# Exponentials that read PSUM in steps and write in order, instead of the reverse, in an attention and gated long-convolution kernel

## The chip, the cores and the metric

The kernel runs on one core of one Trainium2 chip. The metric is the device time of one launch in microseconds (us); before the change the median of three runs is 485.76 us (485.69 to 485.93). The core has a matrix engine (PE), which writes its results to PSUM, and three engines that work on tiles of 128 partitions: ACT (scalar engine: exponentials, copies), DVE (vector engine) and POOL. SP does no arithmetic here; it issues transfers. Each engine takes its own instructions in order, and the engines wait for one another through semaphores.

## The reference

Eight batches, 12 heads, 448 positions, 64 numbers a head. First comes an attention whose softmax has a one added to its denominator (with the maximum m taken out, that one is exp(-m)). Its result, laid out as 448 x 768 per batch, is projected to three streams; the second is convolved along the sequence with a long filter through a Fourier transform, and the three are multiplied and projected again.

```python
# q, k, v: (8, 12, 448, 64)
scores = scale * np.matmul(q, k.transpose(0, 1, 3, 2))
m = np.max(scores, axis=-1, keepdims=True)
e = np.exp(scores - m)
attn = e / (np.sum(e, axis=-1, keepdims=True) + np.exp(-m) + 1e-09)
x = np.matmul(attn, v)                      # then to (8, 448, 768)
x1, x2, x3 = split(x @ w_proj)              # three times 768
x2 = irfft(rfft(x2, axis=1) * rfft(filter_fft, axis=0), n=448, axis=1)
out = (x1 * x2 * x3) @ w_out
```

## The kernel before

**Attention.** The kernel works on pairs of heads: 6 pairs in each of 8 batches, 48 in all, numbered `i`. The maximum is not taken out. For a pair, the 448 keys of each of the two heads fall into three tiles of 128 keys and a rest of 64; the rests of both heads share a fourth tile. `scores(t)` (L767 to L774) lets PE write scores with the keys on the partitions and the queries along the row: for t = 1, 2, 3 two matmuls fill a pair of PSUM banks, one bank for each head, 448 floats in each; for t = 0 one matmul fills one bank with the shared rest. `exps(t)` (L776 to L791) is one ACT instruction that reads these scores from PSUM, applies the exponential and writes bf16 to SBUF: into `e` (896 elements on 128 partitions, a ring of six tiles) for t = 1, 2, 3, and into `er` (448 elements, a ring of two) for t = 0. PE then multiplies `e` and `er` with `vn`, the values with a column of ones (`out_rest`, L811; `out_rests`, L803), taking 128 columns of `e` at a time, that is 128 queries in row order. DVE adds one to the sum, takes its reciprocal and scales (`norm`, L824 to L826), into `xb`.

**Order of the queries.** A row of `e` must hold the queries in row order, 0 to 447. The queries are loaded four rows to a partition (NST = 4), so after transposing, column j * 112 + n of `qT` is query 4n + j. In batches 0 and 1 (`b < NSTAGED`, `staged`) PE transposes q into PSUM, and the copy back (`q_back`, L494 on DVE, once L492 on ACT) reads PSUM in the order (n j), so that `qT` is in row order. In batches 2 to 7 (`loaded`) DMA transposes write `qT` and `kT` (L533, L540) and the columns stay in the order (j n); the scores have that order as well, and the exponentials bring it to row order. The access patterns that do so are all that the change touches.

**The rest.** The scaled result is transposed by DMA (L896; by PE at L905 for most pairs of batch 0). `dense(b)` then folds the sequence into even and odd parts (DVE, L957 and L962), projects (PE L985, copies L997 and L999), applies the Fourier tables (L1012, copies L1020), multiplies by the filter's spectrum (L1026, L1032), transforms back (L1097, copy L1106, DVE L1115 to L1126), computes the two gates (PE L1058, ACT L1070, DVE L1073), multiplies (L1141), projects out (PE L1170, ACT L1182) and stores (SP L1189, L1192).

**Order of the work.** A planner (`Plan`) runs while the kernel is built: every task has an engine, a cost, a wanted time, what it needs and what it makes and which buffers it takes and gives. It emits the tasks in one fixed order for each engine, and gives out PSUM's eight banks; at most two pairs of banks hold scores ("sc") at a time. The exponentials are tasks on ACT with a written-down cost of 0.81 (`e`) and 0.44 (`er`), and those figures are the same in both versions. Attention of later batches is interleaved with `dense` of earlier ones.

**Transfers.** SP issues nearly all loads (q at L562, k and v at L584, the rests at L548), the transposes and the stores, in one order. The loads land in small rooms as float32, and POOL casts them to bf16 (L568 for q, L589 for k, L601 for v); a room is free for the next load after its cast.

Of the kernel before, what the change touches and what calls it, by code (L numbers as in the profile page):

```python
# [21 lines left out]
NST = S // SP  # L22
# [234 lines left out]
def kernel(  # L257
# [97 lines left out]
    def bank(hy):  # L355
        i = plan.banks[hy][0]
        return psum[:, 512 * i : 512 * i + 512]
# [5 lines left out]
    def pair(hy):  # L363
        i = plan.banks[hy][0]
        return psum[:, 512 * i : 512 * i + 1024].rearrange("p (u n) -> p u n", u=2)
# [394 lines left out]
    def attention(i):  # L760
# [15 lines left out]
        def exps(t):  # L776
            if t:
                P["e"][t] = e = es[(3 * i + t - 1) % 6]
                to, of = e[:, 0 : 2 * S], pair(("sc", ("S", i, t)))[:, :, 0:S]
                if b < NSTAGED:  # L780
                    to = to.rearrange("p (u n) -> p u n", u=2)
                else:
                    to = to.rearrange("p (u n j) -> p u j n", u=2, j=NST)
                    of = of.rearrange("p u (j n) -> p u j n", j=NST)
                nc.scalar.activation(to, of, AF.Exp, scale=SCALE)  # L785
            else:
                P["e"][t] = e = er[i % 2]
                to, of = e[:, 0:S], bank(("hy", ("S", i, t)))[:, 0:S]
                if b >= NSTAGED:
                    to, of = to.rearrange("p (n j) -> p j n", j=NST), of.rearrange("p (j n) -> p j n", j=NST)  # L790
                nc.scalar.activation(to, of, AF.Exp, scale=SCALE)  # L791

        def out_banks():
# [52 lines left out]
        for t in range(4):  # L846
            w = tau(i, t / 4 if i or t else 1.0)
            ex = with_rests(i - 1) if t == host else dict(cost=0.0, emit=lambda: None, need=[], make=[], take=[], give=[])
            if t == 0 or b == 0:

                def one(t=t, ex=ex):
                    scores(t)
                    ex["emit"]()

                add("PE", (0.4 if t else 0.19) + ex["cost"], w, one,
                    need=[("kT", i), ("qT", i)] + ([("S", i - 1, 2)] if b else []) + ([] if i or t else ["kT0"]) + ex["need"]
                    + ([("S", i, t - 1) if t > 1 else ("S", i - 1, 3)] if t and (i or t > 1) else []),
                    make=[("S", i, t)] + ex["make"], take=[(ring(t), ("S", i, t))] + ex["take"], give=ex["give"])
            elif (3 * i + t) % 2 == 0:

                old = (i, t - 1) if t > 1 else (i - 1, 3)

                def both(pair=(old, (i, t)), ex=ex):
                    for j, n in pair:
                        T[j]["scores"](n)
                    ex["emit"]()

                add("PE", 0.6 + ex["cost"], tau(old[0], old[1] / 4), both,
                    need=[("kT", old[0]), ("qT", old[0]), ("kT", i), ("qT", i)] + ex["need"]
                    + [("S", old[0], old[1] - 1) if old[1] > 1 else ("S", i - 1, 3)],  # L870
                    make=[("S",) + old, ("S", i, t)] + ex["make"],
                    take=[("sc", ("S",) + old), ("sc", ("S", i, t))] + ex["take"], give=ex["give"])
            add("ACT", 0.81 if t else 0.44, w - 1.0, lambda t=t: exps(t), need=[("S", i, t)],
                make=[("e", i)], take=[("e" if t else "er", (i, t))], give=[(ring(t), ("S", i, t))])
# [465 lines left out]
```

## Time and profile before

| | |
|---|---|
| median of three runs | 485.76 us |
| the profiled execution, its own time | 484.45 us |
| its span, first to last instruction | 482.7 us |
| mean granted clock of PE | 0.975 |
| bytes moved by DMA | 64.43 MB, 133 GB/s over the span |
| attention pair 12 (first of batch 2), first score matmul | 74.0 us |
| last exponential begins | 424.7 us |

The profile is of one execution. A group of instructions is named by its line, its engine and operation, and what it writes and reads; `e<-psum` is an instruction that writes a tile `e` from PSUM. "Busy" is the time in which an engine runs instructions; the last part of such a line is the time in which the engine was idle just before them, and which instruction ended the wait. PEld is PE's loading of weights, which runs beside its matmuls.

### The profile page before, as it was taken

Reading aid. Unit: us, or ns where it says so; the run is one execution under the profiler, and the core shown is the slowest. Engines: PE = TensorE matmul, PEld = TensorE weight load, DVE = VectorE, ACT = ScalarE, POOL = GpSimd, SP = SyncE. Lnnn points to the kernel's source line nnn. Section 1 sums busy time; section 2 is a strip of 40 time slices with the busy share of each in tenths; the row PEclk is TensorE's granted clock in tenths of the full one; section 3 lists DMA queues with packets and bytes.
Section 4 is the critical chain, followed back from the end, with each engine's and each line's share of the span. In section 5 each row is a group of like instructions: output and inputs, shape, how many; then the busy total and the mean of one; then the engine's idle time right before and its main releaser. Section 6 shows DMA issues by size and latency. Waiting matters only on the chain.

```text
span 482.7 us, 9536 instructions
## 1 busy us (share of the span) xinstructions
PE 391.6 (81%) x3700; PEld 242.0 (50%) x3700; DVE 254.0 (53%) x667; ACT 405.3 (84%) x460; POOL 107.4 (22%) x240
## 2 busy tenths in 40 slices
PE   8987996798596777677787987687779887789996
PEld 7655753464343454335453653444346443556653
DVE  5666586556273255392582645435128551387761
ACT  6784889969969999999979699998999989964453
POOL 6736324161333230342313211000000000000000
PEclk9998999899989999999999899899899998999999
DMA  8999968994976995993965403282110113010013
GB/s 233 244 230 238 202 151 189 185 260 105 242 148 170 223 190 151 211 239 73 245 148 139 168 16 116 61 128 67 70 29 2 34 67 98 1 35 1 34 65 132
DMA packets 116333, 64.43 MB, mean 133 GB/s; under 512 B 73085, under 2 KB 112704, under 8 KB 116288
## 3 DMA queue, kind: packets, MB, share of 16 engines
q1 hardware_dynamic: 111568, 58.18, 50.3%
q0 software_dynamic: 4480, 5.41, 6.6%
q8 instruction: 29, 0.48, 0.4%
q10 hardware_dynamic: 240, 0.23, 0.1%
q14 instruction: 16, 0.13, 0.1%
HBM read 43.86 MB, written 11.01 MB: 114 GB/s over the span
## 4 chain that ended last, share of the span: by engine, by line
ACT 41%; PE 36%; issue 8%; DMA 7%; DVE 4%; POOL 2%; SPq 1%; ACTq 0%; POOLq 0%; DVEq 0%
ACT e L785 29%; PE psum L1058 15%; PE psum L985 7%; PE psum L1170 6%; ACT er L791 4%; DMA nat<-in_k_dram 4%; PE psum L811 3%; ACT osb L1182 3%; PE psum L772 2%; DMA nat<-in_q_dram 1%; ACT x L1070 1%; ACT cr L1106 1%; PE psum L1097 1%; ACT xs L1020 1%; PE psum L1012 1%
## 5 line engine op out<-in xcount | busy, mean ns | idle before, releaser
L785 ACT ACTIVATE e<-psum 128x896 bf16<-128x896 f32 x144 | 260.6, 1921 | 15.0 <-PE psum L772 15.0
L1058 PE MATMUL psum<-xT,wproj_bf 128*128 128x448 bf16 x576 | 128.1, 363 | 11.6 <-ACT e L785 7.7
L1058 PEld LDWEIGHTS <-wproj_bf 128*128 128x128 bf16 x576 | 55.3, 100 | 61.6 <-issue 22.3
L985 PE MATMUL psum<-wproj_bf,xf 128*113 128x384 bf16 x384 | 71.1, 331 | 4.1 <-ACT e L785 3.7
L772 PE MATMUL psum<-qT,kT 64*128 64x448 bf16 x288 | 44.5, 358 | 23.9 <-ACT e L785 22.0
L1170 PE MATMUL psum<-wout_bf,yT 128*128 128x384 bf16 x288 | 54.7, 328 | 10.7 <-ACT e L785 6.6
L985 PEld LDWEIGHTS <-xf 128*113 128x113 bf16 x384 | 50.9, 134 | 22.9 <-issue 10.6
L791 ACT ACTIVATE er<-psum 128x448 bf16<-128x448 f32 x48 | 52.6, 1096 | 2.6 <-PE psum L774 2.5
L1026 DVE TENSOR_TENSOR t<-xs,hrs 113x768 bf16<-113x768 bf16 (+1 forms) x64 | 34.7, 577 | 30.5 <-ACT xs L1020 30.5
L824 DVE TENSOR_SCALAR rec<-psum 128x8 f32<-128x8 f32 x48 | 7.8, 162 | 79.7 <-PE psum L811 79.2
L811 PE MATMUL psum<-vn,e 128*128 128x65 bf16 x1152 | 46.7, 197 | 0.0
L1073 DVE TENSOR_TENSOR g<-x,psum 128x448 bf16<-128x448 bf16 x48 | 29.6, 616 | 28.9 <-PE psum L1058 18.4
L1170 PEld LDWEIGHTS <-yT 128*128 128x128 bf16 x288 | 27.7, 98 | 31.8 <-issue 14.8
L811 PEld LDWEIGHTS <-e 128*128 128x128 bf16 x1152 | 41.2, 100 | 3.3 <-issue 0.7
L1070 ACT CAST x<-psum 128x448 bf16<-128x448 f32 x48 | 27.6, 574 | 16.5 <-PE psum L1058 16.4
L1182 ACT COPY osb<-psum 128x384 f32<-128x384 f32 x56 | 28.5, 530 | 14.5 <-PE psum L1170 14.0
L772 PEld LDWEIGHTS <-kT 64*128 64x128 bf16 x288 | 12.1, 94 | 49.2 <-issue 47.6
L568 POOL CAST nat<-nat 112x512 bf16<-112x512 f32 x36 | 22.9, 643 | 56.0 <-DMA nat<-in_q_dram 55.9
L826 DVE TENSOR_TENSOR xb<-psum,rec 128x512 bf16<-128x512 f32 x48 | 33.2, 691 | 1.7
L601 POOL CAST vn<-nat 128x192 bf16<-128x192 f32 x58 | 21.4, 390 | 45.2 <-PE psum L811 42.2
L1020 ACT CAST xs<-psum 113x384 bf16<-113x384 f32 (+1 forms) x64 | 29.4, 527 | 2.0 <-PE psum L1012 1.9
L997 DVE CAST x<-psum 113x384 bf16<-113x384 f32 x32 | 17.6, 551 | 23.9 <-PE psum L985 23.8
(111 smaller groups left out, 446.8 us busy)
## 6 DMA issues: line engine op xcount, KB each, us to landing
nat<-in_q_dram SPq DMA_DIRECT2D x47, 224.0 KB, 4.5
out_dram<-osb SPq DMA_DIRECT2D x24, 384.0 KB, 2.4
nat<-in_k_dram SPq DMA_DIRECT2D x41, 192.0 KB, 4.3
nat<-in_v_dram SPq DMA_DIRECT2D x41, 192.0 KB, 4.7
wproj_bf<-in_moe_w_proj_dram POOLq DMA_DIRECT2D x2, 1152.0 KB, 17.1
rests<-in_k_dram SPq DMA_DIRECT2D x8, 192.0 KB, 4.9
rests<-in_v_dram SPq DMA_DIRECT2D x8, 192.0 KB, 5.1
out_dram<-osb SPq DMA_DIRECT2D x8, 192.0 KB, 2.7
```

Of the source, the lines that this page charges most:

```text
L772: nc.tensor.matmul(sc[:, u, 0:S], kT[b % 2][c, hp, t, :], qT[b % 2][c, hp, :])
L785: nc.scalar.activation(to, of, AF.Exp, scale=SCALE)
L791: nc.scalar.activation(to, of, AF.Exp, scale=SCALE)
L811: nc.tensor.matmul(out_bank(u)[:, n, :], P["e"][1 + t][:, u * S + n * 128 : u * S + n * 128 + 128], vn[b % 2][:, hp, 4 * u + t, :], start= ...
L826: nc.vector.tensor_tensor(W["xb", b][:, hp].rearrange("p n (u d) -> p u n d", u=2), op[:, :, :, 0:DH], rec[:].unsqueeze(3).to_broadcast([1 ...
L985: nc.tensor.matmul(pps[:FQ, :DCH], W["xf", b][:, pg, kt, 0:FQ], wproj_bf[:, kt, D + ch * DCH : D + (ch + 1) * DCH], start=(kt == 0), stop= ...
L1020: nc.scalar.copy(L["xs", par, ch][:K, pg % 2, :], L["Z", pg, ch][:K, :DCH])
L1026: nc.vector.tensor_tensor(t[:K], L["xs", par, ch][:K], h, op=ALU.mult)
L1058: nc.tensor.matmul(p[:, :S], wproj_bf[:, kt, 2 * part * D + dt * 128 : 2 * part * D + (dt + 1) * 128], xT()[:, kt, 0:S], start=(kt == 0), ...
L1070: nc.scalar.copy(L["x1", dt], p[:, :S])
L1170: nc.tensor.matmul(ops[:n, :DCH], y[:, dt, 0:n], wout_bf[:, dt, ch * DCH : (ch + 1) * DCH], start=(dt == 0), stop=(dt == NDT - 1),)
L1182: nc.scalar.copy(L["os", st][:n, ch * DCH : (ch + 1) * DCH], L["O", st, ch][:n, :DCH])
```

## The change

In `exps`, for batches 2 to 7 only, the order in which the instruction walks through its elements is changed. Before, it took the scores in the order in which they lie in PSUM (j, then n) and wrote each at its place in the row, four bf16 elements (8 bytes) after the one before it. Now it takes them in row order (n, then j): it reads PSUM in steps of 112 floats, four to a run, then goes one float on, and writes one element after the other. The same elements arrive at the same places. Batches 0 and 1 are not touched.

```diff
                 if b < NSTAGED:
                     to = to.rearrange("p (u n) -> p u n", u=2)
                 else:
-                    to = to.rearrange("p (u n j) -> p u j n", u=2, j=NST)
-                    of = of.rearrange("p u (j n) -> p u j n", j=NST)
+                    to = to.rearrange("p (u n j) -> p u n j", u=2, j=NST)
+                    of = of.rearrange("p u (j n) -> p u n j", j=NST)
                 nc.scalar.activation(to, of, AF.Exp, scale=SCALE)
             else:
                 P["e"][t] = e = er[i % 2]
                 to, of = e[:, 0:S], bank(("hy", ("S", i, t)))[:, 0:S]
                 if b >= NSTAGED:
-                    to, of = to.rearrange("p (n j) -> p j n", j=NST), of.rearrange("p (j n) -> p j n", j=NST)
+                    to, of = to.rearrange("p (n j) -> p n j", j=NST), of.rearrange("p (j n) -> p n j", j=NST)
                 nc.scalar.activation(to, of, AF.Exp, scale=SCALE)
```

## The prediction

> **What bounds the kernel now.** I began with the page's busy shares and its costliest groups, to see which engine is full and with what.
>
> ```profile
> PE 391.6 (81%) x3700; PEld 242.0 (50%) x3700; DVE 254.0 (53%) x667; ACT 405.3 (84%) x460; POOL 107.4 (22%) x240
> ...
> L785 ACT ACTIVATE e<-psum 128x896 bf16<-128x896 f32 x144 | 260.6, 1921 | 15.0 <-PE psum L772 15.0
> ...
> L772 PE MATMUL psum<-qT,kT 64*128 64x448 bf16 x288 | 44.5, 358 | 23.9 <-ACT e L785 22.0
> ...
> L791 ACT ACTIVATE er<-psum 128x448 bf16<-128x448 f32 x48 | 52.6, 1096 | 2.6 <-PE psum L774 2.5
> ```
>
> ACT and PE are both over 80% busy, and the exponentials (L785, L791) are 313 of ACT's 405 us. The mean of 1921 ns hides two prices, which the view of the single line shows, with the waits that it causes.
>
> ```profile
> L785 ACT ACTIVATE e<-psum x144: 912/2216/2377, 8.5 to 424.7; 128x896 bf16<-128x896 f32 x144
> ...
>   PE psum L772: 22.0, 29
>   PE psum L803: 8.3, 6
>   PE psum L1058: 7.7, 6
> ```
>
> The shortest takes 912 ns and the median 2216 ns, for the same 896 elements. The timeline of ACT says which is which: batches 0 and 1 (before 75 us) are the short ones, batches 2 to 7 the long ones.
>
> ```profile
> 57.87 1.73 ACT L785 ACTIVATE e<-psum 128x896 bf16<-128x896 f32 x2
> 59.47 0.56 ACT L791 ACTIVATE er<-psum 128x448 bf16<-128x448 f32 x1
> 59.90 0.51 ACT L1020 CAST xs<-psum 113x384 bf16<-113x384 f32 x1
> ```
>
> ```profile
> 79.33 1.26 ACT L791 ACTIVATE er<-psum 128x448 bf16<-128x448 f32 x1
> 80.32 0.64 ACT L1106 CAST cr<-psum 128x452 bf16<-128x452 f32 x1
> 80.85 0.54 ACT L1070 CAST x<-psum 128x448 bf16<-128x448 f32 x1
> 81.27 4.18 ACT L785 ACTIVATE e<-psum 128x896 bf16<-128x896 f32 x2
> 85.17 1.08 ACT L1106 CAST cr<-psum 128x452 bf16<-128x452 f32 x2
> ```
>
> From start to next start, an early pair takes 59.47 - 57.87 = 1.60 us (0.80 each), a late pair 85.17 - 81.27 = 3.90 us (1.95 each); an early `er` 0.43 us, a late one 0.99 us. Last I read busy time by stretch: 75 us is where the late exponentials begin, 424.7 us where the last one starts.
>
> ```profile
> 30.00:75.00 45.00, 39.73 (x449) 26.83 (x448) 30.72 (x79) 32.00 (x56) 15.96 (x31) 0.96 0.96 195
> 75.00:139.00 64.00, 49.38 (x429) 28.97 (x430) 33.77 (x84) 55.68 (x57) 21.85 (x45) 0.95 0.94 201
> 139.00:188.50 49.50, 37.30 (x357) 22.43 (x354) 20.23 (x52) 47.64 (x47) 16.42 (x35) 1.00 0.73 173
> 188.50:253.60 65.10, 49.05 (x480) 29.39 (x477) 39.28 (x102) 60.53 (x59) 19.98 (x43) 1.00 0.79 183
> 253.60:424.70 171.10, 136.86 (x1247) 81.68 (x1245) 74.60 (x200) 160.20 (x158) 12.26 (x28) 0.96 0.27 70
> 424.70:482.70 58.00, 52.39 (x357) 32.29 (x355) 35.46 (x93) 26.67 (x55) 0.00 (x0) 1.00 0.17 55
> ```
>
> Columns: length, then busy PE, PEld, DVE, ACT, POOL, then granted clock, DMA share, GB/s. From 75 to 424.7 us (349.7 us) ACT is busy 324.1 us (93%) and PE 272.6 us (78%). Before and after it PE is full: 39.7 of 40.5 us, leaving out 4.5 us in which it waits for a POOL cast (98%), and 52.4 of the 54.1 us up to its last matmul (97%). So the late exponentials set the pace of the middle, and nothing else there.
>
> **Price of a late exponential after the change.** Its write to SBUF becomes contiguous, which the early ones show at 912 and 538 ns. New is the read: PSUM in steps of 112 floats, runs of four. No exponential here reads so. The nearest rows are the copies of `qT` for batches 0 and 1, which read PSUM in the same (n j) order, from bf16 words 112 elements apart, and write plainly.
>
> ```profile
> L492 ACT COPY qT<-psum x1: 567/567/567, 24.6 to 24.6; 128x448 bf16<-128x448 bf16 x1
> ...
> L912 ACT COPY xT<-psum x2: 527/530/532, 32.2 to 36.1; 128x448 bf16<-128x448 bf16 x2
> ...
> L494 DVE COPY qT<-psum x11: 612/624/626, 7.5 to 60.1; 128x448 bf16<-128x448 bf16 x11
> ```
>
> On ACT the scattered read takes 567 ns against 530 for the plain one of the same count: 37 ns per 448 elements, so 74 ns for 896. On DVE it takes 624 against 386 ns (plain copy at L914): 238 ns more, 0.53 ns an element. Low end: nothing more, 0.80 us effective. High end by DVE's row: 0.80 + 0.48 = 1.28 us, and 0.43 + 0.24 = 0.67 us for `er`. A gain below the plain row is excluded, as the element count and the output are the same. I take ACT's own row, rounded to 0.85 and 0.46 us, since it is the same engine and the same order of reading, though one sample and bf16.
>
> [...]
>
> **The change part by part.** Batches 2 to 7 have 36 head pairs: 108 exponentials into `e` and 36 into `er`. ACT loses 108 x (1.95 - 0.85) = 119 us and 36 x (0.99 - 0.46) = 19 us, 138 us together. Nothing else is added, removed or moved: same instructions, same DMAs, same buffers, same waits, and the same order on each engine, since the costs given to the planner stay.
>
> ACT in the middle falls from 324 to 186 us, below PE's 272.6 us. PE is then what takes longest (DVE has 167.9 us, POOL 70.5 us). Of PE's 77 us of idle there, nearly all ends at ACT, L785 above all; in the table of waits some 92 waits of PE end at ACT. Each also stretches the busy time: a lone 448-column matmul (L774) is recorded at 351 ns, but the next one starts 190 ns after it when none waits, so each restart adds 0.16 us: 92 x 0.16 = 15 us. With all of them gone the middle is (272.6 - 15)/0.97 = 266 us; with none of the restarts gone, 272.6/0.97 = 281 us. I take 273.
>
> Sum: 75 us before the middle, 273 us, 58 us after it (the queue of dense work with no exponential in it, PE at 97%) = 406 us of span. The profiled execution took 484.45 us for a span of 482.7 us (+1.75), and the median of the runs is 1.3 us above that: 406 + 3 = 409 us. Own range of this case: 399 + 3 to 414 + 3 us, less a few for an optimistic clock, say 399 to 418 us.
>
> What is late next: score banks come free some 1.1 us earlier, so score matmuls and, through `op` and `xb`, the transposes of x and the stores leave SP's queue earlier. SP issues in order, so the loads behind those entries move forward too, into a stretch in which the DMA engines are already busy for 60.2 + 36.1 + 51.4 = 148 us (shares times lengths, 75 to 253.6 us). PE's need there is 135.7 us. That cover is thin.
>
> **The rivals.** (B) The loads become the bound up to 253.6 us. For: 148 us of DMA against 136 us of PE, and POOL's casts already wait 55.9 us for q and 30.9 us for k. Against: shares up to 1.12 stand in 20 us windows, and the transposes of batches 5 to 7 are issued 40 to 60 us before use, so part of this DMA work can slip past. At its mildest the first half lasts 148 us and the second 136.9/0.97 = 141 us: 75 + 148 + 141 + 58 + 3 = 425 us. If the loads kept today's pace to 253.6 us it would be 456 us.
>
> (C) The read costs on ACT what it costs on DVE. ACT saves 108 x 0.67 + 36 x 0.32 = 84 us; 240 us remain in the middle against 273 of PE, so both are near 90% and wait for each other by turns; at ACT's present 93%, 258 us would do, but PE's order leaves gaps: 285 to 295 us, total 421 to 431 us. For: L494, eleven samples. Against: L492.
>
> (D) Slower: the read in steps costs more than the write in steps. The write costs (2216 - 912)/896 = 1.46 ns an element of 2 bytes; if a 4-byte element read costs twice that, `e` takes 3.5 us and `er` some 2.0 us, 108 x 1.3 + 36 x 0.7 = 166 us more on an engine that is full: some 650 us. It decides from a read price above 1.46 ns an element. Both copies above stay below: 0.08 and 0.53 ns.
>
> (E) The read costs just what the write did, or the order of the instruction's dimensions makes no difference to the engine: 486 us.
>
> **How the numbers follow.** Forecast (A) 64%, B 18%, C 12%, D 3%, E 3%. The predicted time is A's, 409 us. The range goes from 394 us (middle at 258 us, no wait left at all) to 431 us, taking in C and the mild end of B. Faster by over 0.2% (the least a measurement of this kernel can tell from none): A, B and C, 0.94; within it 0.02; slower 0.04.
>
> **What would show it.** L785's median near 0.95 us instead of 2.2 and L791's near 0.57 us confirm the price; 1.4 us is C, 3 us is D. ACT's busy time near 267 us and PE above 90% of the span confirm the new bound; waits of PE should then seldom end at L785. PE waiting for kT or qT from a DMA, or POOL's waits for loads growing, is B. The stretches before 75 us and after the last exponential should keep their lengths. I am wrong if PE's idle in the middle stays above some 25 us though the exponentials are short: then a wait that ACT hides now, in the loads or in DVE's normalising, takes its place.

## The result, and the profile after

The changed kernel takes 386.3 us (median of four runs, 385.65 to 390.55) against 485.85 us for the kernel before on the same chip: a ratio of 0.797, 95% interval 0.791 to 0.803. The forecast was 409 us with a range of 394 to 431. Direction and mechanism were right; the gain is 99.5 us instead of 77, and the time lies below the range.

From the page of the changed kernel: busy times, granted clock and DMA by slice, the shares of the chain that ended last, and the two groups of exponentials.

```profile
PE 364.9 (95%) x3700; PEld 232.4 (60%) x3700; DVE 261.8 (68%) x667; ACT 264.1 (69%) x460; POOL 112.2 (29%) x240
...
PEclk9999999999999999999999999999999999999999
DMA  8999998599999999999999933592302132200214
...
PE 65%; DVE 13%; DMA 12%; ACT 4%; issue 2%; POOL 2%; SPq 2%; POOLq 0%; DVEq 0%; ACTq 0%
...
L785 ACT ACTIVATE e<-psum 128x896 bf16<-128x896 f32 x144 | 126.4, 925 | 21.8 <-PE psum L772 21.6
...
L791 ACT ACTIVATE er<-psum 128x448 bf16<-128x448 f32 x48 | 26.7, 556 | 4.6 <-PE psum L774 4.6
```

The mean of `e` fell from 1921 to 925 ns, that of `er` from 1096 to 556 ns. ACT is down from 405 to 264 us, and PE, with the same 3700 matmuls in the same order, fills 95% of the span. The exponentials now wait for the scores (21.6 us, 15.0 before), and the scores wait for the exponentials for 0.2 us in all (22.0 before). ACT's share of the chain that ended last went from 41% to 4%; the chain's line before the change was:

```profile
ACT 41%; PE 36%; issue 8%; DMA 7%; DVE 4%; POOL 2%; SPq 1%; ACTq 0%; POOLq 0%; DVEq 0%
```

PE's four longest waits after the change:

```profile
PE psum L466 <- POOL k L424: 3.3, 4, 1.6
PE psum L1097 <- DVE g L1073: 2.9, 3, 1.2
PE psum L905 <- DVE xb L826: 1.7, 2, 0.9
PE psum L774 <- DMA qT<-nat: 1.1, 1, 1.1
```

A single wait on an exponential is left, those 0.2 us. Busy time by stretch (length, then busy PE, PEld, DVE, ACT, POOL, then clock, DMA share, GB/s): the middle, which now runs from 74.7 to 328.5 us, and what follows it.

```profile
74.70:328.50 253.80, 247.96 (x2504) 155.10 (x2503) 174.73 (x434) 184.68 (x319) 74.77 (x151) 1.00 0.77 178
328.50:384.40 55.90, 52.03 (x357) 32.08 (x354) 35.17 (x93) 24.58 (x53) 0.00 (x0) 0.98 0.17 57
```

The middle shrank from 349.7 to 253.8 us; 95.9 of the 98.3 us that the span lost are there. What was not expected is PE's busy time in it: 248.0 us, where the same 2504 matmuls were busy for 272.6 us before.

### The profile page after: what moved, and what is told of

It reads as the page before. It is cut to its first block, busy times and chain, and to the rows that moved or that the text cites. A ratio compares the mean times of both kernels' runs of the same rounds, so it can differ in the third digit from the quotient of the medians.

```text
span 384.4 us, 9536 instructions
## 1 busy us (share of the span) xinstructions
PE 364.9 (95%) x3700; PEld 232.4 (60%) x3700; DVE 261.8 (68%) x667; ACT 264.1 (69%) x460; POOL 112.2 (29%) x240
## 4 chain that ended last, share of the span: by engine, by line
PE 65%; DVE 13%; DMA 12%; ACT 4%; issue 2%; POOL 2%; SPq 2%; POOLq 0%; DVEq 0%; ACTq 0%
PE psum L1058 19%; PE psum L985 14%; PE psum L1170 12%; PE psum L811 6%; PE psum L772 5%; DMA nat<-in_k_dram 5%; DMA xT<-xb 3%; DVE t L1026 2%; DMA nat<-in_v_dram 2%; PE psum L1097 2%; PE psum L1012 2%; DMA nat<-in_q_dram 2%; DVE xf L962 2%; DVE yh L1032 2%; ACT e L785 2%
## 5 line engine op out<-in xcount | busy, mean ns | idle before, releaser
L785 ACT ACTIVATE e<-psum 128x896 bf16<-128x896 f32 x144 | 126.4, 925 | 21.8 <-PE psum L772 21.6
L1058 PE MATMUL psum<-xT,wproj_bf 128*128 128x448 bf16 x576 | 122.4, 352 | 0.1
L985 PE MATMUL psum<-wproj_bf,xf 128*113 128x384 bf16 x384 | 69.1, 326 | 1.5 <-DVE g L1073 0.7
L811 PE MATMUL psum<-vn,e 128*128 128x65 bf16 x1152 | 44.7, 194 | 0.0
L1026 DVE TENSOR_TENSOR t<-xs,hrs 113x768 bf16<-113x768 bf16 (+1 forms) x64 | 37.0, 613 | 8.0 <-ACT xs L1020 8.0
L772 PE MATMUL psum<-qT,kT 64*128 64x448 bf16 x288 | 40.8, 355 | 0.6 <-ACT kT L485 0.4
L1182 ACT COPY osb<-psum 128x384 f32<-128x384 f32 x56 | 26.4, 484 | 21.3 <-PE psum L1170 20.0
L1170 PEld LDWEIGHTS <-yT 128*128 128x128 bf16 x288 | 27.5, 98 | 19.2 <-issue 1.5
L1073 DVE TENSOR_TENSOR g<-x,psum 128x448 bf16<-128x448 bf16 x48 | 29.5, 615 | 11.9 <-PE psum L1058 9.5
L999 ACT CAST x<-psum 113x384 bf16<-113x384 f32 x32 | 15.5, 483 | 28.7 <-PE psum L985 28.5
L826 DVE TENSOR_TENSOR xb<-psum,rec 128x512 bf16<-128x512 f32 x48 | 33.2, 691 | 1.7
L1106 ACT CAST cr<-psum 128x452 bf16<-128x452 f32 x48 | 25.3, 547 | 7.0 <-PE psum L1097 6.6
L791 ACT ACTIVATE er<-psum 128x448 bf16<-128x448 f32 x48 | 26.7, 556 | 4.6 <-PE psum L774 4.6
L997 DVE CAST x<-psum 113x384 bf16<-113x384 f32 x32 | 17.5, 550 | 14.1 <-PE psum L985 14.1
```

Of the source, the lines that this page charges most:

```text
L772: nc.tensor.matmul(sc[:, u, 0:S], kT[b % 2][c, hp, t, :], qT[b % 2][c, hp, :])
L811: nc.tensor.matmul(out_bank(u)[:, n, :], P["e"][1 + t][:, u * S + n * 128 : u * S + n * 128 + 128], vn[b % 2][:, hp, 4 * u + t, :], start= ...
L826: nc.vector.tensor_tensor(W["xb", b][:, hp].rearrange("p n (u d) -> p u n d", u=2), op[:, :, :, 0:DH], rec[:].unsqueeze(3).to_broadcast([1 ...
L985: nc.tensor.matmul(pps[:FQ, :DCH], W["xf", b][:, pg, kt, 0:FQ], wproj_bf[:, kt, D + ch * DCH : D + (ch + 1) * DCH], start=(kt == 0), stop= ...
L1026: nc.vector.tensor_tensor(t[:K], L["xs", par, ch][:K], h, op=ALU.mult)
L1058: nc.tensor.matmul(p[:, :S], wproj_bf[:, kt, 2 * part * D + dt * 128 : 2 * part * D + (dt + 1) * 128], xT()[:, kt, 0:S], start=(kt == 0), ...
```

## The experiments

**Reading plainly as well.** In batches 2 to 7 the queries are left in the order in which they lie, so the output's rows are not in order.

```diff
-                    to = to.rearrange("p (u n j) -> p u n j", u=2, j=NST)
-                    of = of.rearrange("p u (j n) -> p u n j", j=NST)
+                    to = to.rearrange("p (u n) -> p u n", u=2)
```

> Batches 2 to 7 read the scores and write the exponentials plainly, in the order in which they lie, so that the queries are not brought into row order; all else is as after the change. Theory (the read in steps costs ACT nothing that matters, PE is the bound): L785 median 912 to 925 ns as after the change (923), L791 540 to 555, time 385 to 388 us. Rival (the read in steps has a price): L785 is shorter here than after the change by more than 20 ns; the time then still stays within 2 us, since PE is the bound.

Measured: 386.9 us (385.7 to 388.0). The groups of ACT, with line numbers one lower than in the changed kernel:

```profile
L784 ACT ACTIVATE e<-psum 128x896 bf16<-128x896 f32 x144 | 126.1, 923 | 23.0 <-PE psum L772 22.9
...
L790 ACT ACTIVATE er<-psum 128x448 bf16<-128x448 f32 x48 | 26.6, 554 | 4.9 <-PE psum L774 4.8
```

923 ns against 925, 554 against 556: reading PSUM in steps of 112 floats costs nothing that shows. The whole price was in the write.

**Each part alone.** First only `er` (L791) has the new order and `e` the old one; then only `e` (L785) has the new one.

```diff
+                    to = to.rearrange("p (u n j) -> p u j n", u=2, j=NST)
+                    of = of.rearrange("p u (j n) -> p u j n", j=NST)
...
+                    to, of = to.rearrange("p (n j) -> p j n", j=NST), of.rearrange("p (j n) -> p j n", j=NST)
```

> Only er (L791) reads in steps and writes plainly; e (L785) writes in steps as before. Theory (time goes with ACT's occupancy while ACT is the bound): ACT saves 36 x 0.56 = 20 us, so 485.8 - 20 = 466 us, 462 to 470; half-clock windows stay. Rival (writes in steps also slow other engines, in proportion to the elements): er has 1/7 of the elements, 1/7 of 99.5 us is 14 us, 472 us.

> Only e (L785) is changed; er (L791) writes in steps as before. Theory (PE is the bound after the change, ACT has room): ACT's middle rises from 185 to 205 us against PE's 248, time 386 to 389 us. Rival (each part of the gain adds up): 20 us come back, 406 us.

Measured: 468.9 us (468.0 to 470.4) with `er` alone; that lies in the theory's interval, but the two theories stood too close together there (the ratio to the kernel before is only known as 0.958 to 0.972) to be told apart. With `e` alone 388.0 us (385.9 to 388.8), as the theory had it and within the spread of the changed kernel: the 20 us of ACT that `er` costs do not show in the time once PE is the bound, and cost 17 us while ACT is.

**ACT kept busy without a write in steps.** Every late exponential of the changed kernel is issued twice.

```diff
+                for _ in range(1 if b < NSTAGED else 2):
                     nc.scalar.activation(to, of, AF.Exp, scale=SCALE)
```

> As after the change, but each late exponential is issued twice, with the same result: ACT is occupied as long as by writes in steps, nearly, without any write in steps. Theory (ACT's occupancy alone makes the waits, and the waits make PE's half-clock windows and restarts): ACT's middle is 185 + 108 x 0.80 + 36 x 0.43 = 287 us, at 93 to 100% full 287 to 308 us: 421 to 442 us; the mean granted clock falls below 0.99 again, with PE busy above 372 us. Rival (the writes in steps themselves slow PE or the others): clock stays at 0.995 or more and PE busy at 365 us, time below 415 us.

Measured: 457.5 us (453.6 to 459.9), above the interval. Four exponentials in a row take 3.55 us from start to next start, 0.89 each and not the 0.80 that I had put. The instructions are no longer than before (mean 923 ns), but a repetition, which writes the same tile, starts some 0.03 us after the first has ended, where two exponentials into different tiles overlap by 0.11 us. ACT is busy 295.4 us instead of 287, in a middle of 324 us: 91% full, where I had reckoned with at least 93% (the kernel before has 93%). What the run was for is clear: PE waits again, its busy time is stretched again (385 us over the span) and its mean clock is 0.987, with no write in steps anywhere. This kernel's waits of PE, and its middle:

```profile
PE psum L772 <- ACT e L786: 14.3, 26, 1.4
PE psum L805 <- ACT e L786: 6.7, 5, 1.4
PE psum L1060 <- ACT e L786: 5.4, 6, 1.4
```

```profile
74.80:398.80 324.00, 266.88 (x2519) 160.88 (x2518) 171.07 (x439) 295.43 (x463) 71.99 (x151) 0.99 0.61 140
```

So ACT's occupancy alone is enough for the longer time. Nor do the rows show that the scattered writes slow another engine: DVE's L826 has a mean of 691 ns before and after the change, and L1073 616 and 615 ns.

**Half the batches.** The change for batches 2 to 4 alone (`b < 5`), and for 5 to 7 alone (`b >= 5`).

```diff
+                    if b < 5:
                         to = to.rearrange("p (u n j) -> p u n j", u=2, j=NST)
                         of = of.rearrange("p u (j n) -> p u n j", j=NST)
+                    else:
+                        to = to.rearrange("p (u n j) -> p u j n", u=2, j=NST)
+                        of = of.rearrange("p u (j n) -> p u j n", j=NST)
```

> The change for batches 2 to 4 alone; 5 to 7 write in steps as before. Theory (each stretch is set by its own bound; half-clock windows only where ACT is the bound): PE reaches the first score matmul of batch 5 at 205.6 us as after the change, and the rest takes 482.7 - 253.6 = 229 us as before: span 435, time 437 us (432 to 442); no half-clock window in 75 to 200 us, some three or four after. Rival (the loads, which ran ahead in the slow kernel, are now late for the second half): more than 445 us.

> The change for batches 5 to 7 alone; 2 to 4 as before. Theory: batch 5 begins at 253.6 us as before, and the rest takes 384.4 - 205.6 = 179 us as after: span 432, time 434 us (429 to 439); half-clock windows only before 255 us. Rival (the second half gains less, since its loads and transposes were not yet ready): more than 440 us.

Measured: 434.2 us (432.4 to 434.4) for the second half, with half-clock windows only before 140 us: as the theory has it. For the first half 441.7 us, at the upper end of the interval, with a wide spread (436.0 to 444.5); the profiled execution is the longest of them. It has one half-clock window where I expected none, at 86 us; whether the shorter executions have it is not known. The timeline of PE there (start, duration, and the wait before it):

```profile
79.88 1.30 PE L1065 MATMUL psum<-xT,wproj_bf 128*128 128x448 bf16 x6
...
85.10 0.36 PE L774 MATMUL psum<-qT,kT 128*128 128x448 bf16 x1 [2.46 <-DMA qT<-nat]
85.30 1.76 PE L1065 MATMUL psum<-xT,wproj_bf 128*128 128x448 bf16 x6
```

PE waited 2.46 us for a DMA transpose, and soon after the same six matmuls took 1.76 instead of 1.30 us. The loads are near the edge, and this wait cost more than its 2.46 us.

**Some exponentials twice.** Of the three late `e` of each pair two (t = 2, 3) are issued twice.

```diff
+                for _ in range(2 if b >= NSTAGED and t > 1 else 1):
                     nc.scalar.activation(to, of, AF.Exp, scale=SCALE)
```

> As after the change, but two of the three late e exponentials of each pair (t = 2, 3) are issued twice: ACT gets 72 x 0.89 = 64 us more in the middle, 249 us, as much as PE's 248. Theory (the two engines then wait for each other by turns; PE's busy time in the middle is 247 us plus 0.16 us for each restart plus half of the half-clock time): 395 to 415 us, with 30 to 70 restarts. Rival (only the fuller engine's sum counts): 386 to 390 us.

Measured: 407.8 us (406.3 to 410.0), as the theory had it. The stretch of this kernel from 75 to 352 us:

```profile
75.00:352.00 277.00, 256.67 (x2517) 157.10 (x2514) 176.69 (x438) 244.56 (x392) 74.58 (x151) 1.00 0.71 164
```

ACT and PE have nearly equal sums here, and the stretch is 20 us longer than PE's and 32 us longer than ACT's: the two wait for each other by turns. The sum of the fuller engine holds only where it is clearly fuller, as in the changed kernel (248 against 185 us).

**More loads.** Two spare loads follow each q load of batches 2 to 7; first 64.5 KB each into two tiles, then 32 KB each into four (shown).

```diff
+    spare = [const.tile([SP, 72], F32, name=f"spare{i}") for i in range(4)]
...
+                ), *(nc.sync.dma_start(
+                    spare[2 * (n % 2) + u][:, :],
+                    q[b, 2 * hp + u].rearrange("(p j) d -> p (j d)", j=NST)[:, 0:72],
+                ) for u in range(2))),
```

> As after the change, but behind each q load of batches 2 to 7 two more loads of 64.5 KB go into spare tiles that nothing reads: 72 x 64.5 KB = 4.6 MB, 19 us of transfer at 250 GB/s, most of it between 75 and 205 us, where the DMA engines already have a share of 1.07 to 1.16. Theory (after the change the loads are just short of being the bound in that stretch): PE waits for kT or qT, 392 to 405 us, with half-clock windows after those waits. Rival (the loads still have room): below 389 us, waits of PE for DMA stay near 1 us.

> As the run before with more loads, but 32 KB each into four spare tiles in turn, so that SP hardly waits for an earlier spare load: 72 x 32 KB = 2.3 MB, 9.5 us of transfer at 250 GB/s, and 72 more issues on SP of some 0.45 us. Theory (the transfers themselves were just short of being the bound): PE waits for kT, qT or xT by more than 5 us, time above 392 us. Rival (the 40 us came from SP's waits for the spare tiles): SP's waits on them fall below 5 us and the time is below 390 us.

Measured: 424.7 us (423.0 to 427.5), far above the interval, and 404.4 us (399.5 to 405.7). Beside the 250 GB/s of both expectations stand 245 GB/s, which the changed kernel moves from 74.7 to 205.6 us at a mean DMA share of 1.10. The first is spoilt as a measure of bandwidth, since SP's queue waited for its own spare tiles:

```profile
SPq L566 <- DMA spare<-in_q_dram: 29.8, 18, 7.6
```

In the second those waits are gone from the top of SP's list, and PE's waits begin with a transfer:

```profile
PE psum L1062 <- DMA xT<-xb: 6.0, 3, 3.7
```

2.3 MB more, 3.6% of all traffic, cost 18 us. Whether that is the transfers or the 72 issues in SP's order (a median of 448 ns each) was not separated. Either way what SP issues stands close behind PE; that it is the next bound is likely, but the two causes were not told apart.

**Two copies from DVE to ACT.** Half of the L997 copies go to ACT, which has room now.

```diff
-            if ch:
+            if ch and pg < 2:
                 nc.vector.tensor_copy(to, of)
```

> As after the change, but two of the four L997 copies of each batch go from DVE to ACT (the planner knows), since ACT now has room and PE's last waits in the middle, 4 to 5 us, end at DVE. Theory (PE at 95% of the span leaves little): 382 to 386 us. Rival (the new order costs more than the waits): above 388 us.

Measured: 386.7 us (384.3 to 387.4), between the two expectations and no difference that the runs can tell from the changed kernel. No version here clearly beats it.

**A bench of steps.** Nothing of the reference is computed. Six instructions of each kind on 448 elements.

```diff
+        nc.scalar.activation(eb[:, 0 : 4 * S : 4], p, AF.Exp, scale=0.125)
...
+            row.rearrange("p (n a c) -> p a n c", a=2, c=2), p.rearrange("p (a n c) -> p a n c", a=2, c=2), AF.Exp, scale=0.125
```

> Nothing of the reference is computed and zeros are stored: a bench of 448-element exponentials and copies, six of each kind in a row, that differ in the step of the read or the write alone. Theory (a bf16 element that does not adjoin the one before it costs a write of its own): steps of 2, 4, 8 and 16 elements all take about 1.26 us against 0.54 plain, runs of two about 0.9, float32 in steps likewise above 0.54; reads in steps of 112 or 4 floats from PSUM 0.54 to 0.56. [...] On DVE a copy that reads in steps takes as long as a plain one, with float32 input.

The groups of ACT and DVE, costliest first. ACT's writes of bf16: L34 plain, L36, L38, L40, L42 in steps of 2, 4, 8, 16 elements, L44 the old order of `er`, L46 runs of two, 8 bytes from run to run. Writes of float32: L50 plain, L52 and L54 in steps of 2 and 4. Plain writes with reads in steps: L56 from PSUM in the new order of `er`, L58 from PSUM every fourth float, L60 from SBUF in the new order. DVE's copies from float32 in PSUM: L64 plain, L66 read in steps, L68 written in steps.

```profile
L40 ACT ACTIVATE eb<-ps 128x448 bf16<-128x448 f32 x6 | 12.9, 2148 | 0.2
L42 ACT ACTIVATE eb<-ps 128x448 bf16<-128x448 f32 x6 | 12.2, 2038 | 0.2
L38 ACT ACTIVATE eb<-ps 128x448 bf16<-128x448 f32 x6 | 7.0, 1160 | 0.2
L44 ACT ACTIVATE eb<-ps 128x448 bf16<-128x448 f32 x6 | 6.9, 1158 | 0.2
L68 DVE CAST eb<-ps 128x448 bf16<-128x448 f32 x6 | 6.9, 1146 | 0.2
L60 ACT ACTIVATE eb<-sf 128x448 bf16<-128x448 f32 x6 | 5.7, 958 | 0.2
L54 ACT ACTIVATE ef<-ps 128x448 f32<-128x448 f32 x6 | 5.7, 955 | 0.2
L36 ACT ACTIVATE eb<-ps 128x448 bf16<-128x448 f32 x6 | 4.0, 667 | 0.2
L66 DVE CAST eb<-ps 128x448 bf16<-128x448 f32 x6 | 3.7, 624 | 0.2
L64 DVE CAST eb<-ps 128x448 bf16<-128x448 f32 x6 | 3.7, 624 | 76.0 <-ACT eb L60 75.8
L52 ACT ACTIVATE ef<-ps 128x448 f32<-128x448 f32 x6 | 3.4, 562 | 0.2
L56 ACT ACTIVATE eb<-ps 128x448 bf16<-128x448 f32 x6 | 3.3, 549 | 0.2
L34 ACT ACTIVATE eb<-ps 128x448 bf16<-128x448 f32 x6 | 3.3, 543 | 0.2
L46 ACT ACTIVATE eb<-ps 128x448 bf16<-128x448 f32 x6 | 3.3, 543 | 0.2
L58 ACT ACTIVATE eb<-ps 128x448 bf16<-128x448 f32 x6 | 3.3, 543 | 0.2
L50 ACT ACTIVATE ef<-ps 128x448 f32<-128x448 f32 x6 | 3.3, 542 | 0.2
```

The theory of the write falls. The price grows with the step (667, 1160, 2148 ns for 4, 8, 16 bytes, 543 plain) and then stays (2038 for 32); but two adjacent elements at a time, 8 bytes apart, take no longer than a plain write (543 ns). Nor do reads from PSUM in steps cost anything that matters (549 and 543 ns). The same read from SBUF takes 958 ns. The bench has no plain read from SBUF beside it; the nearest is L640 of the changed kernel, a sine of 452 floats that lie one after the other in SBUF, at 582 ns, so the steps look dear there. On DVE the plain and the stepped copy, from float32, both take 624 ns, as expected, and the stepped write 1146 ns.

## Why the prediction was right or wrong

**What bounds the kernel: right.** The late exponentials set the pace of the middle, through ACT's occupancy: taken away, PE's waits on them go; put back as repeated plain exponentials, they return.

**The price of a late exponential: right, a little high.** I took ACT's row of the `qT` copy, 74 ns more for 896 elements; it is nothing (925 ns as for the early ones). ACT's middle came to 184.7 us against 186 forecast. Rival C took DVE's 238 ns for the price of reading in steps. The bench shows what that row hid: from float32, which the scores are, a stepped copy on DVE takes as long as a plain one (624 ns). The 386 ns of L914 belong to a plain copy of bf16, so the 238 ns could not be carried over to scores in float32. C, D and E fall with the 925 ns.

**The step that failed: "With all of them gone the middle is (272.6 - 15)/0.97 = 266 us; with none of the restarts gone, 272.6/0.97 = 281 us. I take 273."** It measured 253.8 us. The term that was mis-sized is PE's own work, which I read off its busy time. Busy time held two things that go with the waits. The restarts I had counted, and then took only half of the 15 us: 7.5 us. The other I left out: windows of 3.41 us in which PE's clock is granted at 0.50. The row of the kernel before has them:

```profile
PEclk9998999899989999999999899899899998999999
```

Each 8 is such a window; six of the seven stand in the middle. There six matmuls take 1.78 us, and 1.14 us a little later (timeline of PE before the change):

```profile
265.03 1.78 PE L1170 MATMUL psum<-wout_bf,yT 128*128 128x384 bf16 x6 [2.24 <-ACT e L785]
...
269.17 1.14 PE L1170 MATMUL psum<-wout_bf,yT 128*128 128x384 bf16 x6
```

Six windows of 3.41 us at a clock of 0.50 make 20.5 us; by my estimate half of that, some 10 us, is busy time that is no work. I had this in front of me, a mean clock of 0.95 to 0.97 in the middle, and named it only as "a few" us of the range. The same middle (from the first pair of batch 2 to the last exponential, the same matmuls) in the runs, counted in their traces; the last column is 247 + 0.16 x restarts + half of the half-clock time:

| kernel | PE busy, us | PE idle, us | restarts | half clock, us | 247 + ... |
|---|---|---|---|---|---|
| before | 272.9 | 77.1 | 104 | 20.5 | 273.9 |
| `er` only | 266.8 | 68.1 | 94 | 10.2 | 267.1 |
| all twice | 265.6 | 56.8 | 96 | 6.8 | 265.8 |
| batches 2 to 4 | 262.9 | 44.9 | 61 | 13.7 | 263.6 |
| batches 5 to 7 | 258.7 | 42.9 | 54 | 6.8 | 259.0 |
| some twice | 255.9 | 19.4 | 51 | 0.0 | 255.2 |
| `e` only | 249.1 | 5.4 | 12 | 0.0 | 248.9 |
| plain reads | 248.5 | 5.8 | 10 | 0.0 | 248.6 |
| after | 248.0 | 5.8 | 9 | 0.0 | 248.4 |

The 247 is fitted; the 0.16 is the figure of the prediction, and the half follows from the clock of 0.50. All nine agree within 1.0 us. (A least-squares fit of the nine rows that leaves these two free gives 0.17 us and 0.41.) In the two runs with more loads the sum comes out 5.3 and 1.7 us too high, because PE stood idle in part of their half-clock windows: of 37.5 and 13.7 us it was busy in 28.9 and 11.4. With half of those the sum is within 1.1 us there too. So PE's work in the middle is some 247 us, and 26 of its 273 busy us went with its waits, nearly all of which ended at ACT. The error of 19.2 us in the middle is about 10 us of half clock, 7.5 us of restarts taken half, and 2 us of idle time overrated. The stretches before and after gave 2.4 us more, 130.6 instead of 133 us, and the step from span to median, put at 3 us, was 1.9.

**What is late next, and rival B: nearly.** The loads did move into a full stretch: the DMA shares there read 1.07 to 1.16 in the changed kernel. They held PE up for 1.1 us, not for 16. The 148 us of DMA time were no floor: the first half of the middle, 74.7 to 205.6 us, lasted 130.9 us at a mean share of 1.10. Shares above 1 stood in the profile before as well, one stretch of 20 us (80 to 100 us) with 1.15, above the 1.12 that the prediction names as the most. But the runs with more loads, and the 2.46 us wait in the run with batches 2 to 4, show how little was missing. The count of DMA time against PE time put the two too close to tell, and that was so.

## What to carry to other kernels

Where two layouts differ and a scalar-engine instruction must bridge them on its way out of PSUM, let it read in steps and write adjacent elements: here a median of 923 against 2216 ns for the same work. When an engine is about to become the bound, do not take its busy time for its work: subtract the restart after each wait (0.16 us by estimate) and what the reduced clock adds (half of 20.5 us here), which went with the waits: 104 restarts became 9, and 20.5 us at half clock became none. Then look at the engine or queue that runs close behind, since where two sums are nearly equal (245 and 257 us here) the time is longer than either (277 us).

## What the runs showed of the hardware that was not expected

The price of ACT's write in steps depends on more than the distance in bytes. At 8 bytes from one write to the next, bf16 elements one by one take 1160 ns, pairs of bf16 543 ns and float32 562 ns; at 16 bytes bf16 takes 2148 and float32 955 ns. Which part of the write path this is was not settled.

Windows of 3.41 us at a clock of 0.50 came with waits of PE of three kinds: on exponentials written in steps (20.5 us of such windows in the middle before the change), on plain ones issued twice (6.8 us), and on a DMA (the wait of 2.46 us in the run with batches 2 to 4). In each trace the windows lie on a fixed grid of 3.41 us; in the kernel before they begin at 40.08, 91.28, 132.24, 265.36, 309.74, 347.28 and 405.31 us. Take the stretches of this grid in the middles of all twelve kernels (the bench apart). Of those at full clock 26 were followed by one at half, and in each of the 26 PE was idle for 1.36 to 3.41 us. In the other 952 it was idle for 1.90 us at most. In the kernel before alone PE was idle for 1.80 to 2.29 us in the six that a window followed, and for 1.90 us at most in the others. By these counts a window goes with the idle time that falls into one stretch, though the two ranges overlap, and not with the number of waits: `some twice` has 51 restarts and 19.4 us of idle time in its middle and no window, while with more loads (64.5 KB each) the windows add up to 37.5 us at 31 us of idle time.
